# Attention and a mixture of experts in one kernel: order of the attention and item work fixed by the program, weight buffers with fixed uses

## The chip, the core and the metric

One Trainium2 chip, one core. The metric is the device time of one execution in microseconds (us). Engines: PE (TensorE, matrix products), DVE (VectorE), ACT (ScalarE), POOL (GpSimd, which issues the indirect transfers), SP (SyncE, which issues the other transfers). PEld stands for PE's weight loads.

## What is computed

```python
def _attn_ref(q, k, v, tau):            # B, N, C = 4, 3648, 256
    qn = q / (np.linalg.norm(q, axis=1, keepdims=True) + 1e-06)
    kn = k / (np.linalg.norm(k, axis=1, keepdims=True) + 1e-06)
    s = kn.transpose(0, 2, 1) @ qn / tau
    s = s - s.max(-1, keepdims=True)
    a = np.exp(s)
    a /= a.sum(-1, keepdims=True) + 1e-09
    return (v @ a).astype(np.float32)
...
g_idx = np.argmax(x @ w_group, axis=1)  # x: 14592 x 256; 4 groups of 4 experts
...
h = np.maximum(xg[mask_e] @ w1[g, e], 0.0)      # 256 -> 1024
ye = h @ w2[g, e]                               # 1024 -> 256
out[tok_idx] = combined[:, None] * ye
```

Attention is over channels: the score matrix of a batch is 256 x 256, summed over 3648 rows. Each row of its output is a token; the token goes to the best expert of its best group, weighted by both softmax values. Everything is float32.

## The kernel before, in words

**Attention.** A batch is 28 tiles of 128 rows and a remainder of 64; four tiles make a unit, so a batch has 8 units (`GPB`), the last with the remainder alone, and the kernel 32. For a unit of scores, `s_load` brings q and k, `s_split` splits one of the four tiles (`SPLIT`) into a rounded part and its rest and squares all of them on ACT (`sq`), `s_mm` multiplies into `sacc` (L207), and `s_add` adds the squares on DVE (`sqa`). The split tile takes three products of rounded values (`qkhi`, `qklo`) where the other tiles take one full-precision product. For a unit of output, `x_load` brings v, `x_tr` transposes it on PE (`vtr`, L284), ACT rounds it to `vth`, DVE forms the rest `vtl`; `x_mm` makes six products a tile (`xmm`, L303) with the softmax matrix (`ahi`, `alo`), and ACT copies them to `xs`, a ring of ten buffers. The softmax matrix is widened by 20 columns, so that the same products give the routing logits `L`.

**Softmax and routing** are chains of small instructions that go from engine to engine, written as generators. `softmax(b)`: DVE sums the squares (`ssq`), PE sums over partitions (`nps`), ACT takes the root, DVE scales the scores, ACT the exponential, PE transposes (`atp`) and multiplies with the routing weights (`awp`), ACT and DVE make `ahi` and `alo`. `routing(b, j0, j1)` takes a range of tiles (`RANGES`): DVE finds group and expert, counts by a scan (`inc`, `rs`), PE sums the counts over partitions (`pp`, L359), DVE forms slot numbers `si`; `scatter` then lets POOL write each tile's 128 tokens to their slots in `x_sorted` (L405), 116 in all, with a `pause` (L139) behind each.

**Order.** The loop over `t` issues unit t of the scores and unit t - 10 of the output (`XOFF`); from t = 32 on only output is left. A step of a generator is issued at four places a loop (`sstep`) or by `advance`. Up to t = 31 only POOL takes the program's order; the other engines' order is made by a list scheduler, which places instructions by priority. From t = 32 to step 2 of the items all engines take the program's order, and behind that SP and POOL alone.

**Items.** An item is one expert with 512 tokens; there are 28 (`NBIG`), and the 24 from item 4 on (`host`) also carry a quarter of a group of smaller token blocks (`qmm`, `qacc`). The first `KPRE` = 4 items come from an early table (`tables_pre`), made once the first two batches and the range before `PRE` are counted; the others from `tables_rest`, when every token is counted. SP fetches an early item's rows with a plain transfer, POOL those of the others with a gather (`gather`, L478), for which all scatters and the clearing of the empty slots (L557) must be done. Weights of 1 MB (w1, w2) and of 512 KB (for the small blocks) go through a ring of three raw buffers (`raw_tile`); ACT and DVE split them into `wh` and `wl` (`split_w`). An item has eight steps f: `ffn1` makes six products into `hmm` (L793), ACT and DVE make `hh` and `hl`, and `ffn2` multiplies those of two steps ago (`lag`) into `yacc` (L809). POOL sends the results out (L819). Rows of early items are transposed on PE (`split_x`), those of the others on DVE (`turn_x`), both during the item before.

## Time and profile before

| | us |
|---|---|
| median of 3 runs | 962.31 (960.9 to 963.89) |
| the profiled execution | 958.63 |
| its span, first to last instruction | 956.9 |
| PE busy | 924.3 |
| DVE busy | 750.0 |
| ACT busy | 477.3 |
| POOL busy | 332.2 |

The span has four stages by time: scores alone to about 57 us, scores and output side by side to about 200, output alone to about 252, items to 945. Busy time of an engine is the time in which it executes an instruction; an engine with idle time before an instruction waited for another engine or for a transfer, and the views name which.

### The profile page before, as it was taken

Reading aid. Unit: us, or ns where it says so; the run is one execution under the profiler, and the core shown is the slowest. Engines: PE = TensorE matmul, PEld = TensorE weight load, DVE = VectorE, ACT = ScalarE, POOL = GpSimd, SP = SyncE. Lnnn points to the kernel's source line nnn. Section 1 sums busy time; section 2 is a strip of 40 time slices with the busy share of each in tenths; the row PEclk is TensorE's granted clock in tenths of the full one; section 3 lists DMA queues with packets and bytes.
Section 4 is the critical chain, followed back from the end, with each engine's and each line's share of the span. In section 5 each row is a group of like instructions: output and inputs, shape, how many; then the busy total and the mean of one; then the engine's idle time right before and its main releaser. Section 6 shows DMA issues by size and latency. Waiting matters only on the chain.

```text
span 956.9 us, 17625 instructions
## 1 busy us (share of the span) xinstructions
PE 924.3 (97%) x6238; PEld 809.5 (85%) x6238; DVE 750.0 (78%) x1511; ACT 477.3 (50%) x748; POOL 332.2 (35%) x425
## 2 busy tenths in 40 slices
PE   7999999988899999999999999999999999999995
PEld 6889899878799988888888888888888888888884
DVE  6989978798899977777877777778777877887731
ACT  6777768447554444444444444444443444444421
POOL 0003878878787322222111311232223222322121
PEclk9999999999999999999999999999999999999998
DMA  8866778448684545555566555666666666556500
GB/s 314 313 243 224 238 269 295 144 147 287 202 296 153 176 159 210 208 210 211 213 219 212 202 213 204 222 229 221 222 223 230 222 222 220 197 212 211 200 25 26
DMA packets 105585, 201.90 MB, mean 211 GB/s; under 512 B 10035, under 2 KB 64059, under 8 KB 105488
## 3 DMA queue, kind: packets, MB, share of 16 engines
q1 hardware_dynamic: 89056, 156.12, 47.6%
q0 software_dynamic: 14944, 44.54, 12.1%
q8 instruction: 51, 0.84, 0.3%
q14 instruction: 46, 0.38, 0.1%
q10 hardware_dynamic: 1488, 0.02, 0.1%
HBM read 170.33 MB, written 31.39 MB: 211 GB/s over the span
## 4 chain that ended last, share of the span: by engine, by line
PE 80%; DVE 6%; POOL 4%; issue 4%; DMA 2%; ACT 2%; POOLq 0%; SPq 0%; DVEq 0%; ACTq 0%
PE yacc L809 32%; PE hmm L793 32%; PE sacc L207 7%; POOL x_sorted L405 3%; PE qacc L913 2%; PE qmm L896 2%; PE xmm L303 2%; DMA qkraw<-in_k 2%; DVE sqa L191 1%; POOL pad L139 1%; PE vtr L284 1%; DMA x_sorted<-xs,si 1%; DVE vtl L286 1%; ACT sq L183 1%; PE qtr L903 1%
## 5 line engine op out<-in xcount | busy, mean ns | idle before, releaser
L797 ACT ACTIVATE hh<-hmm 128x512 fp32r<-128x512 f32 x224 | 133.4, 596 | 298.0 <-PE hmm L793 284.5
L819 POOL DMA_INDIRECT out<-ys,ids x112 | 111.1, 992 | 479.1 <-ACT ys L816 449.1
L809 PE MATMUL yacc<-wh,hh 128*128 128x256 f32 x896 | 256.2, 286 | 0.1
L809 PE MATMUL yacc<-wh,hl 128*128 128x256 f32 x896 | 252.5, 282 | 0.0
L809 PE MATMUL yacc<-wl,hh 128*128 128x256 f32 x896 | 252.0, 281 | 0.0
L798 DVE SCALAR_TENSOR_TENSOR hl<-hmm,hh 128x512 fp32r<-128x512 f32 x224 | 153.4, 687 | 85.9 <-ACT hh L797 84.3
L809 PEld LDWEIGHTS yacc<-wh,hh 128*128 128x128 f32 x896 | 168.7, 188 | 24.4 <-issue 15.0
L793 PE MATMUL hmm<-xth,wh 128*128 128x512 f32 x448 | 177.3, 396 | 0.0
L793 PE MATMUL hmm<-xth,wl 128*128 128x512 f32 x448 | 177.0, 395 | 0.0
L793 PE MATMUL hmm<-xtl,wh 128*128 128x512 f32 x448 | 176.8, 395 | 0.0
L809 PEld LDWEIGHTS yacc<-wl,hh 128*128 128x128 f32 x896 | 169.0, 189 | 8.2
L687 DVE STREAM_TRANSPOSE xt<-xg 32x256 f32<-32x256 f32 x384 | 167.2, 435 | 6.5 <-DMA xg<-x_sorted,ix_big 0.2
L640 DVE TENSOR_TENSOR wl<-wraw,wh 128x1024 fp32r<-128x1024 f32 x112 | 134.9, 1223 | 46.9 <-ACT wh L639 45.6
L809 PEld LDWEIGHTS yacc<-wh,hl 128*128 128x128 f32 x896 | 168.5, 188 | 0.0
L405 POOL DMA_INDIRECT x_sorted<-xs,si x116 | 135.6, 1169 | 56.3 <-issue 29.3
L639 ACT ACTIVATE wh<-wraw 128x1024 fp32r<-128x1024 f32 x112 | 116.2, 1055 | 74.1 <-DMA wraw<-in_moe_w 50.5
L793 PEld LDWEIGHTS hmm<-xth,wl 128*128 128x128 f32 x448 | 84.1, 188 | 19.9
L793 PEld LDWEIGHTS hmm<-xtl,wh 128*128 128x128 f32 x448 | 84.2, 188 | 11.0 <-DVE xtl L668 0.3
L793 PEld LDWEIGHTS hmm<-xth,wh 128*128 128x128 f32 x448 | 84.2, 188 | 9.7
L207 PE MATMUL sacc<-qkraw 128*128 128x256 f32 (+1 forms) x352 | 85.2, 388 | 6.0 <-DMA qkraw<-in_k 6.0
L207 PEld LDWEIGHTS sacc<-qkraw 128*128 128x128 f32 (+1 forms) x352 | 65.0, 193 | 14.6 <-DMA qkraw<-in_q 5.9
L303 PE MATMUL xmm<-ahi,vth 128*128 128x276 f32 (+1 forms) x232 | 69.7, 302 | 3.2 <-ACT ahi L263 1.8
(233 smaller groups left out, 1212.3 us busy)
## 6 DMA issues: line engine op xcount, KB each, us to landing
wraw<-in_moe_w SPq DMA_DIRECT2D x56, 1024.0 KB, 7.2
wraw<-in_moe_w SPq DMA_DIRECT2D x96, 512.0 KB, 5.4
vr<-in_v SPq DMA_DIRECT2D x28, 512.0 KB, 4.2
qkraw<-in_q SPq DMA_DIRECT2D x27, 512.0 KB, 4.8
qkraw<-in_k SPq DMA_DIRECT2D x27, 512.0 KB, 5.7
xg<-x_sorted SPq DMA_DIRECT2D x4, 544.0 KB, 4.0
x_sorted<-xs,si POOLq DMA_INDIRECT x116, 4.0
out<-ys,ids POOLq DMA_INDIRECT x112, 3.6
```

The costliest lines, as they stand in the source:

```text
L207: PE.matmul(d["acc"][:, c, :], kt[:rows, 1, cs], qt[:rows, 0, :], start=d.pop("first", True) and c == 0, stop=(g == NG), skip_group_check= ...
L303: PE.matmul(mm[:rows, :NE], vt[:, c, j * P:j * P + rows], at[:, c, :], start=(n == 0), stop=(n == 5))
L405: ins = POOL.indirect_dma_start(out=xs_d, out_offset=bass.IndirectOffsetOnAxis(ap=si[:rows, j:j + 1], axis=0), in_=xs[:rows, t, 0:RW].bitc ...
L639: ACT.activation(whs[n][:, s], raw[:, s], AF.Copy)
L640: DVE.tensor_tensor(wls[n][:, s], raw[:, s], whs[n][:, s], ALU.subtract)
L687: ins = DVE.transpose(xt[qs_, :, :, rs], xg[:, :, :, qs_])
L793: PE.matmul(mm, wt[:, c, fs], xt[:, c, :], start=(n == 0), stop=(n == 5))
L797: d["hh"] = ACT.activation(hh, mm, AF.Relu)
L798: d["hl"] = DVE.scalar_tensor_tensor(hl, mm, 0.0, hh, ALU.max, ALU.subtract)
L809: PE.matmul(a, ht[:, tsl], wt[:, f, :], start=(f == 0 and t % 2 == 0 and n == 0), stop=(f == 7 and n == 2), skip_group_check=True)
L819: ins = POOL.indirect_dma_start(out=out, out_offset=bass.IndirectOffsetOnAxis(ap=d["ids"][:, t:t + 1], axis=0), in_=ys[:, t, :], in_offset ...
L896: PE.matmul(mm[r, :], qs["xT"][q % 2][:, c, r], qs["w", p][:, c * 512:(c + 1) * 512], start=(c == 0), stop=(c == 1), tile_position=(0, p * ...
```

## The change

All five engines take the program's order from the start to the end of the items. The loop over attention is a list of steps (t, x): output starts at t = 13 (`FIRST`), two steps with output alone stand after t = 13 and t = 15 (`ALONE`), and unit 31 of the output, the short one, goes before unit 30. Within a step, tiles of scores and output alternate, and behind each a `hook` counts; a generator's `yield n` waits for n hooks. Softmax goes into one line of generators (`small`), routing and tables into another (`rgens`); `take` and `give` hand the one small PSUM buffer around. Squares and their additions are halved and placed between tiles. Units 9 to 12 don't split a tile. Softmax adds its squares instead of reducing, makes the column norms as four single columns and spreads one of them by a product with a diagonal matrix (`dq`), and scales scores on ACT. Logits are copied by ACT.

The items keep their products. `KPRE` is 3, `PRE` (2, 16), batch 2 is routed in three ranges, item 3 is fetched by a gather and still transposed on PE, and outputs are held (`outs`) until the first gathers are issued. Raw buffers have fixed uses: from item 4 on, both weights of an item go through buffer 0 and the small blocks' through 1 and 2. `PLAN` says what DVE and ACT do for the next item behind `ffn1` (0) and `ffn2` (1) of each step.

```diff
-KPRE = 4
+KPRE = 3
+FLIP = 4
...
-RANGES = [[(0, 16), (16, NJ)], [(0, 16), (16, NJ)], [(0, 16), (16, 20), (20, NJ)], [(0, 16), (16, NJ)]]
+RANGES = [[(0, 16), (16, NJ)], [(0, 16), (16, NJ)], [(0, 8), (8, 16), (16, NJ)], [(0, 16), (16, NJ)]]
...
-PRE = (2, 20)
+PRE = (2, 16)
...
+VLOADS = 3
+UNSPLIT = (9, 10, 11, 12)
...
-XOFF = GPB + 2
-TM = US
-TURNS = (0, 1, 2, 3)
+FIRST = GPB + 5
+ALONE = (13, 15)
+HOP = 4
+MANUAL = 24
...
+    hooks, held = [0], [False, 0]
+
+    def take():
+
+        if held[0] or hooks[0] < held[1]:
+            return False
+        held[0] = True
+        return True
+
+    def give(n):
+        held[:] = [False, hooks[0] + n]
...
     def softmax(b):
...
+        hop = HOP if b in (0, B - 1) else HOP + 2
+        sqa = d["sqa"]
         ssq = ap_.tile([P, 2, C], F32, name="ssq", bufs=1)
-        DVE.tensor_reduce(ssq, d["sqa"].rearrange("p t j c -> p t c j"), AX.X, ALU.add)
-        yield
+        DVE.tensor_tensor(sqa[:, :, 0:2, :], sqa[:, :, 0:2, :], sqa[:, :, 2:4, :], ALU.add)
+        DVE.tensor_tensor(ssq, sqa[:, :, 0, :], sqa[:, :, 1, :], ALU.add)
+        yield hop
+        ACT.activation(tmp1, onesf[:, 0:1], AF.Sqrt)
+        while not take():
+            yield 1
...
+        for i in range(4):
+            PE.matmul(nps[:, C + i:C + i + 1], ssq[:, i // 2, (i % 2) * P:(i % 2 + 1) * P], onesf[:, 0:1],
+                      start=(i == 0), stop=True, skip_group_check=True)
+        rn = ap_.tile([P, 4], F32, name="rn4", bufs=1)
+        ACT.activation(rn, nps[:, C:C + 4], AF.Sqrt)
+        ACT.activation(tmp1, zero[:, 0:1], AF.Exp)
+        give(2)
+        yield 1
...
+        dq = ap_.tile([P, 2, P], F32, tag="rn", name="dq", bufs=1)
+        DVE.tensor_tensor(dq, ident.unsqueeze(1).broadcast_to([P, 2, P]),
+                          rn[:, 0:2].unsqueeze(2).broadcast_to([P, 2, P]), ALU.mult)
+        yield hop
+        while not (d.get("scored") and take()):
+            yield 1
+        nps = ps.tile([P, 512], F32, tag="misc", name="nps", bufs=1)
+        PE.matmul(nps[:, 0:C], onesf, dq.rearrange("p c n -> p (c n)"), start=True, stop=True, skip_group_check=True)
         sm = ap_.tile([P, 2, C], F32, name="sm", bufs=1)
         for c in range(2):
-            DVE.scalar_tensor_tensor(sm[:, c, :], d["acc"][:, c, :], rn[:, C + c:C + c + 1], rn[:, 0:C],
-                                     ALU.mult, ALU.mult)
+            ACT.activation(sm[:, c, :], d["acc"][:, c, :], AF.Copy, scale=rn[:, 2 + c:3 + c])
+        yield 1
+        DVE.tensor_tensor(sm, sm, nps[:, 0:C].unsqueeze(1).broadcast_to([P, 2, C]), ALU.mult)
+        give(hop)
...
             DVE.tensor_scalar(ax[:, c, 0:C], sm[:, c, :], se[:, c:c + 1], None, ALU.mult)
-        yield
-        yield
+        yield hop
+        while not take():
+            yield 1
...
         DVE.tensor_copy(ax[:, :, C:NE], awp[:, 0:2 * NL].rearrange("p (c n) -> p c n", c=2))
+        give(hop)
+        yield 2
         ahi = ap_.tile([P, 2, NE], F32R, name="ahi")
         alo = ap_.tile([P, 2, NE], F32R, name="alo")
         ACT.activation(ahi, ax, AF.Copy)
+        yield 1
         DVE.tensor_tensor(alo, ax, ahi, ALU.subtract)
+        yield 2 if b < B - 1 else 1
         d["ahi"], d["alo"] = ahi, alo
```

The line of routing, the raw buffers, the hooks and the loop over attention:

```diff
+        yield 2
+        ez = wide("ez", NL)
+        ACT.activation(ez, z, AF.Exp)
+        yield HOP if (b, j0) < (2, 16) else HOP + 3
+        while not take():
+            yield 1
...
+    turn = [0]
+
+    def raw_tile(n=None):
+
+        n = turn[0] % 3 if n is None else n
+        turn[0] += 1
+        return wp.tile([P, 2048], F32, tag=f"wraw{n}", name="wraw", bufs=1)
...
-        d[which + "r"] = t = raw_tile().rearrange("p (c f) -> p c f", c=n)
+        d[which + "r"] = t = raw_tile(0 if turn[0] > 9 else None).rearrange("p (c f) -> p c f", c=n)
...
-    ms.enter_context(tc.manual_schedule(engines={ET.Pool}))
-
-    rgens = []
+    ms.enter_context(tc.manual_schedule(engines={ET.Pool, ET.SP, ET.Activation, ET.PE, ET.DVE}))
...
+    class Line:
...
+                if r is not None:
+                    self.wait = r
+                    return
+                self.gens.pop(0)
+
+        def hook(self):
+            self.wait -= 1
+            if self.wait <= 0:
+                self.step()
+
+    small, rgens = Line(), Line()
+    wp = tb_pre = tb_big = tb_pc = tb_sub = nsub = None
...
+    def hook():
+        hooks[0] += 1
+        small.hook()
+        rgens.hook()
...
+    steps, x = [], 0
+    for t in range(US):
+        steps.append((t, x if t >= FIRST else None))
+        x += t >= FIRST
+        if t in ALONE:
+            steps.append((None, x))
+            x += 1
+    steps += [(None, u) for u in (*range(x, UX - 2), UX - 1, UX - 2)]
...
+    for n, (t, x) in enumerate(steps):
+        nx = steps[n + 1][1] if n + 1 < len(steps) else None
+        if t is not None and t + LOADS < US:
...
+        if x is not None and x % GPB == 0:
+            while "alo" not in st[x // GPB]:
+                small.hook()
+        if x == UX - 4:
+            while wp is None:
+                hook()
+            fetch_x(items[0], tb_pre, 0)
+        while x is not None and pend_of(x - RING + (x >= UX - 4)):
+            hook()
+            scatter(2)
         if nx is not None:
-            with ahead(t >= US):
-                x_tr(nx)
...
+            x_tr(nx, 0)
+        done = len([a for a in steps[:n + 1] if a[0] is not None])
+        upto = min(US - 1, done + (n >= FIRST))
+        for j in range(GJ):
+            if t is not None and j < rows_of(t % GPB)[1]:
+                s_tile(t, j)
+                if t % GPB == NG:
+                    st[t // GPB]["scored"] = True
+                hook()
+            if j == 0 and nx is not None:
+                x_tr(nx, 1)
+                hook()
+            if x is not None and j < rows_of(x % GPB)[1]:
+                x_tile(x, j)
+                hook()
+            if j == (2 if x is not None else 0) and t is not None and t + 1 < US:
+                s_split(t + 1)
+            if j == 1 and x == UX - 2:
                 split_x(items[0])
...
+            if j % 2 == 0 and squares and squares[0][0] <= upto:
+                s_square(*squares.pop(0))
+            if j % 2 == 1 and adds and adds[0][0] <= upto:
+                u, h = adds.pop(0)
+                s_add(u, h)
+                if h and u % GPB == NG:
+                    small.gens.append(softmax(u // GPB))
+                    small.step()
+            if fetched is None and wp is not None:
+                fetched = n
+            if fetched is not None and n >= fetched + 2 and x != UX - 1 and j % 2 and quarters:
+                split_w(0, *quarters.pop(0), of=4)
```

The items:

```diff
+        outs.append((d, t))
+        if fetched is None:
+            send()
...
-        if i < KPRE:
-            fetch_x(d, tb, k)
         if weights:
             fetch_big(i, "w1")
             fetch_big(i, "w2")
-        if i >= KPRE:
+        if i != KPRE + 1:
             fetch_x(d, tb, k)
...
+    rgens.gens += [routing(B - 1, *RANGES[B - 1][-1]), tables_rest()]
...
-        t = raw_tile()
+        t = raw_tile(1 + half)
...
+    PLAN = {(0, 0): range(0, 2), (0, 1): range(2, 4), (1, 0): ("w1", 0), (2, 0): ("w1", 1), (2, 1): range(4, 7),
+            (3, 0): range(7, 9), (3, 1): range(9, 12), (4, 0): range(12, 14), (4, 1): range(14, 16),
+            (5, 0): ("w2", 0), (5, 1): ("w2", 1), (6, 0): "x", (6, 1): "ids"}
+
+    def ready(i, f, half):
+
+        what = PLAN.get((f, half))
+        if what == "x":
+            split_turned(items[i])
+        elif what == "ids":
+            ids_of(items[i])
+        elif isinstance(what, tuple):
+            split_w(i, what[0], (what[1],))
+        elif what:
+            turn_x(items[i], what)
+
...
-                if i + 2 == KPRE:
-                    advance(1000)
-                    scatter(NJ)
-                    tb_big, tb_pc, tb_sub, nsub = tables_rest()
-                get(i + 2, weights=jn is None)
+                if i + 2 != KPRE:
+                    get(i + 2, weights=jn is None)
...
             ffn1(items[i], f)
+            if quarters:
+                split_w(0, *quarters.pop(0), of=4)
+            if FLIP <= i + 1 < NBIG:
+                ready(i + 1, f, 0)
...
+        if n == 8 * KPRE - 2:
+            split_x(items[KPRE])
+        if n < len(seq) and FLIP <= seq[n][0] + 1 < NBIG:
+            ready(seq[n][0] + 1, seq[n][1], 1)
...
+        hook()
+        if n == 15:
+            while tb_big is None:
+                advance(1)
+        if tb_big is not None and fetched is not None:
+            get(KPRE)
+            fetch_x(*where(KPRE + 1))
+            fetched = None
+            send()
+        scatter(8)
```

**First place of the order: PE, the routing product `pp` and the transposes `atp` of batch 3's softmax, shortly after the last unit of scores.** `vtr` are transposes of v, `xmm` output products, `tri` and `onesb` the constant operands of `pp`. Before:

```order
L303 MATMUL xmm<-ahi,vtl 128x276
L284 MATMUL vtr<-ident,vr 128x64 x2
L359 LDWEIGHTS tri
L359 MATMUL pp<-rs,tri 128x16
L360 LDWEIGHTS onesb
L360 MATMUL pp<-rs,onesb 128x16
L248 MATMUL atp<-ident,ax 128x128 x4
L303 MATMUL xmm<-ahi,vth 128x276
```

After:

```order
L351 MATMUL xmm<-alo,vth 128x276
L409 LDWEIGHTS tri
L409 MATMUL pp<-rs,tri 128x16
L410 LDWEIGHTS onesb
L410 MATMUL pp<-rs,onesb 128x16
L351 MATMUL xmm<-ahi,vth 128x276
...
L333 MATMUL vtr<-ident,vr 128x64 x2
...
L351 MATMUL xmm<-ahi,vtl 128x276
L351 MATMUL xmm<-alo,vth 128x276
L296 MATMUL atp<-ident,ax 128x128 x4
L351 MATMUL xmm<-ahi,vth 128x276
```

`pp` and `atp` stood one behind the other, right behind two transposes; now 12 output products, two transposes and 12 more products stand between them, and the left-out rows are those products.

**Second place: POOL, from the last scatters to the first gathers (`xg`) of items that come from the late table.** `zero` clears the empty slots, `out` is the output, `qxg` the small blocks. Before:

```order
L404 IOTA xs 128x1
L405 DMA x_sorted<-xs,si 238080x272
L139 MEMSET pad 128x256
L819 DMA out<-ys,ids 14592x256 x8
L557 DMA x_sorted<-zero,endi 238080x272
L478 DMA xg<-x_sorted,ix_big 128x1088
L819 DMA out<-ys,ids 14592x256 x4
L478 DMA xg<-x_sorted,ix_big 128x1088
L478 DMA qxg_4538<-x_sorted,ix_pc 128x272
```

After:

```order
L458 IOTA xsr 128x1
L459 DMA x_sorted<-xsr,si 238080x272
L145 MEMSET pad 128x256
L617 DMA x_sorted<-zero,endi 238080x272
L535 DMA xg<-x_sorted,ix_big 128x1088 x2
L933 DMA out<-ys,ids 14592x256 x12
L535 DMA xg<-x_sorted,ix_big 128x1088
L535 DMA qxg_4578<-x_sorted,ix_pc 128x272
```

Eight outputs stood between the last scatter and the clearing; now the clearing and two gathers follow the last scatter, and twelve outputs come behind them.

## Rows read from the trace of the kernel before

**Rows 1.** The page: the span, and busy time of PE (us, share, instructions).
```profile
span 956.9 us, 17625 instructions
...
PE 924.3 (97%) x6238; PEld 809.5 (85%) x6238; DVE 750.0 (78%) x1511; ACT 477.3 (50%) x748; POOL 332.2 (35%) x425
```

**Rows 2.** Stages: length, busy PE, PEld, DVE, ACT, POOL (instructions), clock, DMA share, GB/s.
```profile
57.00:200.00 143.00, 136.95 (x951) 128.07 (x950) 121.28 (x246) 99.05 (x177) 94.46 (x135) 1.00 0.66 223
200.00:252.00 52.00, 43.74 (x319) 40.43 (x317) 44.37 (x148) 31.01 (x72) 41.40 (x69) 0.97 0.64 213
280.00:945.00 665.00, 664.91 (x4526) 571.23 (x4524) 512.22 (x972) 289.85 (x434) 167.54 (x172) 1.00 0.57 200
```

**Rows 3.** Waits of PE: waiting line, awaited line, us in all, times, longest.
```profile
PE pp L359 <- DVE rs L357: 4.8, 6, 1.6
PE vtr L284 <- DVE vtl L286: 2.4, 3, 1.3
PE xmm L303 <- ACT ahi L263: 1.8, 1, 1.8
PE xmm L303 <- ACT xs L306: 1.4, 2, 0.9
```

**Rows 4.** The chain that ended last, attention: start us, us, what.
```profile
5.97 29.36 PE sacc L207 x145
...
120.85 3.08 PE xmm L303 x24
...
124.81 3.30 PE sacc L207 x18
```

**Rows 5.** Timeline of PE, 45 to 47 us: start us, us, instruction.
```profile
45.60 1.04 PE L284 MATMUL vtr<-ident,vr 128*128 128x128 f32 x8
46.40 0.36 PE L207 MATMUL sacc<-qkhi 128*128 128x256 f32 x1
```

**Rows 6.** Groups by line, 0 to 252 us: small products, busy us and mean ns.
```profile
L257 PE MATMUL awp<-wcat,aT 128*128 128x20 f32 x32 | 4.1, 262 | 0.1
...
L248 PE MATMUL atp<-ident,ax 128*128 128x128 f32 x16 | 3.3, 310 | 1.8 <-DVE ax L242 1.1 <-DVE carry L364 0.6
```

**Rows 7.** The same chain, the first item.
```profile
251.97 3.06 PE hmm L793 x12
...
263.78 1.44 PE yacc L809 x12
...
269.44 1.44 PE yacc L809 x12
```

**Rows 8.** Timeline of PE, 208 to 211 us.
```profile
208.25 0.43 PE L303 MATMUL xmm<-alo,vth 128*128 128x276 f32 x1
...
210.78 0.36 PE L303 MATMUL xmm<-ahi,vth 128*128 128x276 f32 x1
```

**Rows 9.** Timeline of POOL: scatters, the clearing of empty slots, the first gather.
```profile
85.95 2.26 POOL L405 DMA_INDIRECT x_sorted<-xs,si  x1 [19.48 <-DVE si L372]
...
189.40 1.00 POOL L405 DMA_INDIRECT x_sorted<-xs,si  x1 [0.28 <-POOL xs L402]
...
190.89 0.98 POOL L405 DMA_INDIRECT x_sorted<-xs,si  x1 [0.16 <-issue]
...
297.98 0.94 POOL L405 DMA_INDIRECT x_sorted<-xs,si  x1 [1.77 <-issue]
...
310.59 0.90 POOL L557 DMA_INDIRECT x_sorted<-zero,endi  x1 [0.30 <-DVE ids L491]
315.84 1.06 POOL L478 DMA_INDIRECT xg<-x_sorted,ix_big  x1 [4.34 <-DVE tst L458]
```

**Rows 10.** DMA issues: KB each, median us from issue to landing.
```profile
wraw<-in_moe_w SPq DMA_DIRECT2D x56, 1024.0 KB, 7.2
...
xg<-x_sorted,ix_big POOLq DMA_INDIRECT x24, 7.9
```

**Rows 11.** Timeline of PE, the last product.
```profile
944.98 0.28 PE L809 MATMUL yacc<-wh,hl 128*128 128x256 f32 x1
```

More of the change, by code (lines that the diff above doesn't have):

```diff
@@ L307, in x_mm @@
[L307 to L312 removed]
+        if j == 0:
+            rows_at[b, g] = ring(GJ, NE, name="xs") if g < NG else rp.tile([P, 1, NE], F32, name="xsr", bufs=2)
+        xs = rows_at[b, g]
+        mm = ps.tile([P, 512], F32, tag="mm", name="xmm", bufs=3)
+        n = 0
+        for c in range(2):
+            for vt, at in ((x["th"], d["ahi"]), (x["tl"], d["ahi"]), (x["th"], d["alo"])):
+                PE.matmul(mm[:rows, :NE], vt[:, c, j * P:j * P + rows], at[:, c, :],
+                          start=(n == 0), stop=(n == 5))
+                n += 1
@@ L314, in bc @@
+        ACT.activation(xs[:rows, j, :], mm[:rows, :NE], AF.Copy)
+        if j == nj - 1:
+            ACT.activation(d["L"][:rows, g * GJ:g * GJ + nj, :], xs[:rows, :nj, C:NE], AF.Copy)
+    scatters, pend, now, rows_at, early, gone = [], [], [0], {}, [], set()
     def bc(x, n):
@@ L539, in tables_rest @@
         DVE.tensor_tensor(small, small, r, ALU.mult)
+        yield 1
         nb = r16("nb")
```

450 lines of the change are left out of this document (207 added, 243 removed).

## The prediction

> **What bounds the kernel now.** I read four views: the page's shares, the stages, the waits of PE, and the chain with the timeline for the pace of single products.
>
> The page shows PE busy for 924.3 us of a span of 956.9 [rows 1]. That average covers stages with different limits. From 280 to 945 us, the items, PE is busy 664.91 of 665 us: nothing that moves a wait can gain there. From 57 to 200 us, attention with scores and output side by side, it is busy 136.95 of 143, so 6.05 us are idle; from 200 to 252 us, where only the output half of attention is left, 43.74 of 52, so 8.26 us are idle [rows 2]. These 14.3 us are what a better order can win back for certain. DVE is the next engine, with 121.28 busy of 143.
>
> The waits say who causes them [rows 3]: the small product `pp` of the routing stands behind DVE's `rs` for 4.8 us in six places, the transposes of v behind DVE's `vtl` for 2.4, the first `xmm` of a batch behind ACT's `ahi` for 1.8, `xmm` behind ACT's evacuation `xs` for 1.4. So PE waits mostly where a link of a chain of small instructions stands directly behind the link that feeds it.
>
> A second estimate comes from the pace of the products. A full unit of scores takes 3.30 us, its 24 output products 3.08 [rows 4], its eight transposes 46.40 - 45.60 = 0.80 [rows 5]. 28 full units make 28 x 7.18 = 201.0; the four remainders are one tile instead of four, a quarter of 7.18 each, 7.2 together. The six groups of small products (softmax and routing) are led by 4.1 and 3.3 us of busy time [rows 6]; the others are smaller, so together at most 4.1 + 5 x 3.3 = 20.6, and since their records overlap perhaps half. With item 0's eight transposes (0.8) PE has 219 to 230 us of work between its first product at 5.97 and the first product of item 0 at 251.97 [rows 4, 7]. That stretch is 246.0 us, so 16 to 27 us of it are not work; I take the middle, 21.
>
> One piece of it has no wait: from 208.25 to 210.78 [rows 8] eleven intervals of `xmm` take 2.53 us, 0.23 each, against 3.08 / 24 = 0.128 elsewhere. [...]
>
> **The change, part by part.**
>
> *Order of attention.* All five engines now follow the program. Output of batch b starts later against its scores (13 units behind, then 11 after two output-only steps, instead of 10), and the links of softmax and routing are released one by one between products ("hooks"). The first order excerpt shows it: `pp` and `atp` stood in a row, now 12 output products, two transposes and 12 more stand between. 12 products of 0.128 are 1.5 us, about the longest single wait on `rs` (1.6) [rows 3]. I therefore take the waits on `rs`, `ahi` and the like as gone, half of the 2.4 on `vtl` as staying, because the transposes still follow each other through two PSUM buffers, and all of the 1.4 on `xs`: 14.3 - 1.2 - 1.4 = 11.7 us gained. Bounds: 0 and 14.3.
> [...]
> *The rest of the 21*: 21 - 14.3 - 1.3 = 5.4 us of slower pace without a named wait. I take half, 2.7; bounds 0 and 11 (27 minus the same).
> *Moved work.* Squares and their additions are cut in half and given places; copying the logits goes from DVE to ACT; the reduction of four square sums becomes two additions. DVE loses work and ACT gains some; neither is PE's, and ACT is busy 99.05 of 143 [rows 2], so I cost this at nothing. If that cover is gone, it shows as PE waiting for ACT's `xs`.
> *Added products.* Four units no longer split their last tile (two full-precision products for six rounded ones), the norms take five products for three, and batch 2 is routed in three ranges instead of two. Nearest rows: 4.1 us for 32 records of `awp` [rows 6], 0.13 each; some 20 more records are 2 to 3 us if nothing is saved, 0 if the dropped ones weigh as much. I take 1.0.
> *The strict order itself.* DVE is busy 85% of 57 to 200 us [rows 2] and would be nearer 90% in a shorter stage, so a link can come later than its place. PE waited 1.6 us at worst for `rs` [rows 3] with ready products behind it; links that stand 1.5 us or more apart leave little of that, so I cost the fixed places themselves at nothing, and the other outcome is a rival below. [...]
>
> *Item 3's rows.* Three instead of four items come from the early table, so item 3 now waits for every scatter. The second excerpt shows POOL: the late rows of an item are now fetched before any output is sent, where eight outputs stood ahead. PE needs item 3's rows at the second-last step of item 2, 22 steps of 2.83 us after the first `hmm` ((269.44 - 263.78) / 2) [rows 7], so 62 us later: 251.97 - 15.7 + 62 = 298. When do they come? Scatters follow each other every 190.89 - 189.40 = 1.49 us at best; 116 of them from 85.95 end at 259 plus some 5 for their 28 iotas; before they ended at 298.9 because POOL also waited for routing [rows 9]. From the clearing of the empty slots at 310.59 to the gather at 315.84 are 5.3 us, and a gather lands 7.9 us after its issue [rows 9, 10]. Arrival: 264 + 13 = 277 at best, 299 + 13 = 312 with POOL's old timetable. The wait is 0 to 14 us; with routing earlier by the gain above, POOL's timetable lies near the middle (295), so I take 1.5.
>
> *Items.* From item 0 on PE gets the same products in the same sequence; 2.83 us a step stays [rows 7], and DVE and ACT have room beside it (512.22 and 289.85 of 665 [rows 2]). *End:* the last product at 944.98 [rows 11] and the 12 us to the end of the span are untouched.
>
> Sum: -11.7 - 1.3 - 2.7 + 1.0 + 1.5 = -13.2 us. The profiled execution took 958.63 us (span 956.9); the median shown is 962.31, 3.7 higher. I apply the difference to the median: 962.3 - 13.2 = 949.1 us (against the profiled execution 945.4).
>
> **The rivals.**
>
> *The scatters set the pace.* POOL keeps most of its old timetable, item 3's rows come at about 306, and PE waits 8 us instead of 1.5: 949 + 7 = 956 us. For it: POOL is busy 94.46 of 143 and 41.40 of 52 [rows 2], the most loaded it ever is. Against: it also waited for routing, which comes earlier.
>
> *Nothing gained: one late operand holds the queue.* [...] The waits vanish at `pp` and come back at `xs` and `vtl`: the 13 us are given back, 962 us, give or take 4. For it: DVE's 85%. [...] Against: the waits of DVE and ACT on each other are not in PE's list now.
>
> *Slower: one raw buffer for both weights of an item.* Now w1 and w2 of the items beside small tokens go through the same raw buffer. w2's load can start only when w1's second half has been split at step 2, and is needed at step 5: three steps, 8.5 us [rows 7], against 7.2 us from issue to landing [rows 10]. PE itself is two steps ahead of its need, 5.7 us more. It decides from a landing of 14 us on, twice the median, which would take two loads queueing behind each other. A wait of 1 us in each of 24 items makes +24: 949 + 24 = 973 us. Against it: loads of 7.2 us.
>
> **How the numbers follow.** Forecast 949.1: chance 0.68. Scatters 956: 0.16. Nothing gained 962: 0.09. Slower 973: 0.07. About 0.3% (2.9 us, so 959.4 and 965.2) is what a measurement of this kernel can tell from no change. The forecast is faster (0.68); of the scatters' case 0.13 is faster, 0.03 lies within; of the third 0.02 is faster, 0.05 within, 0.02 slower; the fourth is slower. Sum: faster 0.83, same 0.08, slower 0.09. Range: all waits gone and all slower pace recovered is 14.3 + 1.3 + 11 = 26.6 less 1 = 25.6, so 937 at the low end; the high end takes in the scatters' case and its bound, 960.
>
> **What would show it.** Right: first `hmm` near 236; 57 to 252 us with PE idle under 4 us until then; no wait on `rs` or `ahi` in PE's list; granted clock 1.00 throughout; item steps still 2.83; 28 items in the same 693 us. Wrong: a wait at item 3's transposes or first products (scatters), long waits on `xs` or `vtl` (queue), ACT's `wh` waiting for `wraw` with `hmm` standing behind (buffer).

## The result, and the profile after

The changed kernel takes 949.17 us (median of 4 runs, 948.94 to 950.34); before, with one run more, 962.07 (960.9 to 963.89). The ratio is 0.9867, 95% interval 0.9849 to 0.9884. Forecast were 949.1 us, and 937 to 960.

The two profiled executions are nearer to each other: 949.24 against 958.63, 9.4 us, where the medians differ by 12.9. The profiled execution of before is none of the four whose times are listed, and it is quicker than all of them. The other 3.5 us are the subject of the first experiment.

The page of the changed kernel, span and busy time [rows 1]:

```profile
span 947.5 us, 17624 instructions
...
PE 924.7 (98%) x6246; PEld 809.5 (85%) x6246; DVE 749.5 (79%) x1502; ACT 484.1 (51%) x822; POOL 336.1 (35%) x426
```

Its stages, columns as in [rows 2], the later cuts moved to where these stages now end:

```profile
57.00:200.00 143.00, 140.72 (x980) 131.15 (x979) 115.62 (x254) 108.87 (x229) 84.07 (x128) 1.00 0.66 231
200.00:236.00 36.00, 33.76 (x264) 31.93 (x263) 29.89 (x97) 25.54 (x68) 30.62 (x53) 1.00 0.63 209
236.00:280.00 44.00, 43.30 (x284) 38.92 (x284) 41.78 (x110) 25.36 (x47) 38.60 (x62) 1.00 0.67 229
280.00:930.00 650.00, 650.00 (x4422) 557.26 (x4421) 518.43 (x970) 282.08 (x424) 177.37 (x169) 1.00 0.60 205
```

PE is idle for 2.28 us from 57 to 200 (6.05 before) and for 2.24 us from 200 to 236, and the granted clock is 1.00 in all four stages; 0.97 is gone. The items are as full as they were. The waits of PE that are left [rows 3]:

```profile
PE vtr L333 <- DVE vtl L335: 2.7, 4, 1.6
PE pp L409 <- DVE rs L401: 1.3, 3, 0.5
PE atp L296 <- DVE carry L414: 0.8, 1, 0.8
...
PE xmm L351 <- ACT xs L354: 0.2, 1, 0.2
```

`rs` fell from 4.8 to 1.3, `xs` from 1.4 to 0.2, `ahi` is gone; `vtl` stays, 2.7 for 2.4. The chain of waits of this execution reaches back only to 922 us, so PE's timeline has to give the stages' ends [rows 7, 11]: the first product of item 0, then the last product.

```profile
243.41 0.40 PE L897 MATMUL hmm<-xth,wh 128*128 128x512 f32 x1
```
```profile
936.31 0.28 PE L913 MATMUL yacc<-wh,hl 128*128 128x256 f32 x1
```

First `hmm` in the timeline is at 243.41 (before 251.81; the chain's entry at 251.97 begins 0.16 later), the last product at 936.31 instead of 944.98: 8.4 of the 9.4 us came from before the first item, 0.3 from the items, and 0.7 from behind the last product (11.2 us to the end of the span for 11.9). POOL, from the last scatter to the first gather [rows 9], and item 3's transposes on PE:

```profile
296.13 0.94 POOL L459 DMA_INDIRECT x_sorted<-xsr,si  x1 [1.98 <-issue]
...
297.56 0.93 POOL L617 DMA_INDIRECT x_sorted<-zero,endi  x1 [0.16 <-DVE tp L490]
301.39 1.05 POOL L535 DMA_INDIRECT xg<-x_sorted,ix_big  x1 [2.90 <-issue]
```
```profile
307.51 1.04 PE L764 MATMUL xtr<-ident,xg 128*128 128x128 f32 x8
```

Item 3's rows are transposed right when PE gets there. The first four items take 90.59 us (before 91.27), the other 24, up to the start of the last product, 602.31 (601.90).

### The profile page after: what moved, and what is told of

Its sections match the earlier page's. It is cut to its first block, busy times and chain, and to the rows that moved or that the text cites. A ratio compares the mean times of both kernels' runs of the same rounds, so it can differ in the third digit from the quotient of the medians.

```text
span 947.5 us, 17624 instructions
## 1 busy us (share of the span) xinstructions
PE 924.7 (98%) x6246; PEld 809.5 (85%) x6246; DVE 749.5 (79%) x1502; ACT 484.1 (51%) x822; POOL 336.1 (35%) x426
## 5 line engine op out<-in xcount | busy, mean ns | idle before, releaser
L933 POOL DMA_INDIRECT out<-ys,ids x112 | 128.0, 1143 | 453.8 <-ACT ys L920 422.8
L736 DVE TENSOR_TENSOR wl<-wraw,wh 128x1024 fp32r<-128x1024 f32 (+1 forms) x116 | 134.8, 1186 | 15.5 <-ACT wh L735 15.5
L459 POOL DMA_INDIRECT x_sorted<-xs,si x112 | 122.3, 1092 | 64.9 <-DVE qklo L182 38.1
L735 ACT ACTIVATE wh<-wraw 128x1024 fp32r<-128x1024 f32 (+1 forms) x116 | 115.5, 1023 | 0.5 <-DMA wraw<-in_moe_w 0.5
L224 PE MATMUL sacc<-qkraw 128*128 128x256 f32 (+1 forms) x368 | 93.1, 389 | 6.4 <-DMA qkraw<-in_k 6.4
L224 PEld LDWEIGHTS sacc<-qkraw 128*128 128x128 f32 (+1 forms) x368 | 66.9, 194 | 14.6 <-DMA qkraw<-in_q 6.0
L351 PE MATMUL xmm<-ahi,vth 128*128 128x276 f32 (+1 forms) x232 | 75.7, 326 | 0.2 <-ACT xs L354 0.2
```

Source lines behind the costliest of these rows:

```text
L224: PE.matmul(d["acc"][:, c, :], kt[:rows, 1, cs], qt[:rows, 0, :], start=d.pop("first", True) and c == 0, stop=(g == NG), skip_group_check= ...
L351: PE.matmul(mm[:rows, :NE], vt[:, c, j * P:j * P + rows], at[:, c, :], start=(n == 0), stop=(n == 5))
L459: ins = POOL.indirect_dma_start(out=xs_d, out_offset=bass.IndirectOffsetOnAxis(ap=si[:rows, j:j + 1], axis=0), in_=xs[:rows, t, 0:RW].bitc ...
L735: ACT.activation(whs[n][:, s], raw[:, s], AF.Copy)
L736: DVE.tensor_tensor(wls[n][:, s], raw[:, s], whs[n][:, s], ALU.subtract)
L933: ins = POOL.indirect_dma_start(out=out, out_offset=bass.IndirectOffsetOnAxis(ap=d["ids"][:, t:t + 1], axis=0), in_=d["ys"][:, t, :], in_o ...
```

## The experiments

Kernels of one group ran on the same chip. Times are medians in us, ratios are to the kernel before on that chip; the last three columns are from the profile: the start of the first `hmm`, then the length of items 0 to 3 and of items 4 to 27, up to the start of the last product.

| kernel | us | ratio (95%) | hmm | 0-3 | 4-27 |
|---|---|---|---|---|---|
| before, shown | 962.07 | | 251.81 | 91.27 | 601.90 |
| changed, shown | 949.17 | 0.9867 (0.9849 to 0.9884) | 243.41 | 90.59 | 602.31 |
| *group 1* b_again | 964.51 | 0.9998 (0.9970 to 1.0026) | 255.47 | 92.48 | 606.29 |
| a_again | 953.73 | 0.9883 (0.9856 to 0.9909) | 244.40 | 92.86 | 602.67 |
| a_nohop | 1018.86 | 1.0563 (1.0534 to 1.0592) | 301.56 | 99.44 | 603.42 |
| b_order | 1036.9 | 1.0735 (1.0705 to 1.0765) | 327.74 | 92.74 | 605.04 |
| *group 2* a_sched | 963.54 | 0.9946 (0.9912 to 0.9981) | 246.58 | 97.90 | 603.25 |
| a_lag | 983.67 | 1.0156 (1.0084 to 1.0227) | 268.81 | 94.29 | 603.22 |
| a_ring | 965.1 | 0.9938 (0.9898 to 0.9978) | 254.40 | 94.58 | 606.44 |
| a_spread | 961.8 | 0.9915 (0.9890 to 0.9939) | 248.00 | 97.68 | 603.38 |
| *group 3* a_ctl | 948.74 | 0.9866 (0.9836 to 0.9896) | 242.71 | 90.45 | 602.31 |
| a_nopause | 947.69 | 0.9855 (0.9825 to 0.9884) | 241.70 | 90.44 | 602.35 |
| a_r1 | 948.45 | 0.9860 (0.9831 to 0.9890) | 244.02 | 90.44 | 602.35 |
| *group 4* a_kpre4 | 956.47 | 0.9898 (0.9868 to 0.9927) | 247.53 | 91.61 | 604.15 |

The kernel before took 965.7, 970.0, 961.79 and 967.06 us on the four chips. In groups 2 and 4 the changed kernel itself wasn't run; there kernels of the group are compared, or a trace is read by itself, and a difference to the changed kernel on another chip is only a hint.

### Both kernels once more: b_again, a_again

No edit.

> The kernel before once more, unchanged, for a second profile of it. Theory A (the profiled execution of before was a quick one of an unsteady kernel): the runs lie at 960 to 964 again, and this profile shows first hmm 1 to 4 us later than 251.97, with the extra time as waits of PE in attention, the items again in 693 us. Theory B (the 3.5 us between that profile and its median lie elsewhere, in the items or outside the span): first hmm within 0.5 us of 251.97, and the items or the time around the span longer.

> The changed kernel once more, unchanged. Theory A (fixed places make the time steady): first hmm within 0.5 us of 243.41, all runs within 1.5 us of 949.2. Theory B (its runs only happened to agree): first hmm moves by 1 us or more, runs spread over 3 us or more as those of before do.

Before: its runs lie at 960.4 to 971.93, not within A's 960 to 964, and this execution loses 3.7 us in attention (first `hmm` 255.47) and 4.4 us in items 4 to 27. Of the 3.7 us, 1.8 are idle time of PE and 2.0 a longer busy time, with a granted clock of 0.94 from 200 us to first `hmm` (0.97 in the execution shown before). Theory A holds for attention in size, B for the items, which A had taken as fixed. So the kernel before does vary on one chip, by 11.5 us; whether the profiled execution shown before was quick by that or by its chip is open, as its chip is not on record. Three waits tell where the items lose. First ACT's in the execution shown before, then ACT's in this one (both from 330 to 930 us), then PE's in this one from 300 on:

```profile
ACT wh L639 <- DMA wraw<-in_moe_w: 49.4, 32, 3.3
```
```profile
ACT wh L639 <- DMA wraw<-in_moe_w: 85.9, 35, 5.1
```
```profile
PE yacc L809 <- DVE ys L818: 2.4, 4, 1.3
```

ACT's rounding of weights waits for their load, for 49.4 us in the quick execution and for 85.9 in this one. DVE's `wl` waits with ACT, 43.8 and 57.5 us (from 330 to 940 us); with a longest wait of 3.3 us none of that reaches PE, whose list from 300 us on is empty there; with 5.1 it does, and PE waits 2.4 us for `ys`. The longest of these four waits of PE, followed back in b_again on ACT, DVE and PE:

```profile
650.21 1.06 ACT L639 ACTIVATE wh<-wraw 128x1024 fp32r<-128x1024 f32 x1 [4.46 <-DMA wraw<-in_moe_w]
```
```profile
651.30 1.23 DVE L640 TENSOR_TENSOR wl<-wraw,wh 128x1024 fp32r<-128x1024 f32 x1 [4.83 <-ACT wh L639]
...
659.94 0.88 DVE L818 TENSOR_SCALAR ys<-yacc,xg 128x256 f32<-128x256 f32 x2
```
```profile
660.87 0.39 PE L809 MATMUL yacc<-wh,hh 128*128 128x256 f32 x1 [1.27 <-DVE ys L818]
```

Between the two rows of DVE it works without a wait, so the late load reaches PE by way of `wh`, `wl` and `ys`. In the three profiles of the changed kernel no such wait of ACT stands in the list. Between the profiles of b_again and a_again, on one chip, 11.1 us lie before first `hmm`, 3.6 in items 4 to 27, and items 0 to 3 are 0.4 us longer in the changed kernel.

Changed: neither theory as stated. The runs stay within 2.2 us of each other, but at another level (952.8 to 954.99); first `hmm` comes 1.0 us later, items 0 to 3 take 2.3 us longer. The place is item 3, whose first products on PE stand behind ACT's rounding of its transposed rows. The timelines of PE, then of ACT, in a_again:

```profile
314.27 0.49 PE L897 MATMUL hmm<-xth,wh 128*128 128x512 f32 x1 [1.20 <-issue]
315.00 0.50 PE L897 MATMUL hmm<-xtl,wh 128*128 128x512 f32 x1 [0.23 <-issue]
```
```profile
310.79 0.60 ACT L765 ACTIVATE xth<-xtr 128x512 fp32r<-128x512 f32 x1 [2.91 <-PE xtr L764]
313.62 0.60 ACT L765 ACTIVATE xth<-xtr 128x512 fp32r<-128x512 f32 x1 [2.24 <-remote]
```

The transposes stand at 308.51 in the records, with no wait for `xg` ahead of them, yet ACT begins only at 310.79 and 313.62. The second half of `xth` is done at 314.22, and the product that reads it starts at 314.27: that PE waits for ACT here is shown, why ACT was late is not. The trace names no releaser that explains it.

### Distance and order: a_nohop, b_order, a_sched

a_nohop (the loop that waits for a batch's matrix now runs both lines):

```diff
-                    self.wait = r
+                    self.wait = 1
...
-        held[:] = [False, hooks[0] + n]
+        held[:] = [False, 0]
...
-                small.hook()
+                hook()
```

> The changed kernel with every link of softmax, routing and tables released at the next hook instead of some hooks later: program order, lag and products stay, the distance between links goes. Theory A (the gain is distance between links): PE's waits on rs, ax, alo and the like come back, 5 to 8 us more of PE idle between 57 us and first hmm, which moves from 243.4 to 248 to 251; 954 to 957 us. Rival (program order and the larger lag do it, the distance is worth nothing): first hmm within 1.5 us of 243.4, 948 to 951 us.

b_order, an edit of the kernel before:

```diff
-        if t == TM:
+        if t == 0:
             ms.close()
             ms.enter_context(tc.manual_schedule(engines={ET.Pool, ET.SP, ET.Activation, ET.PE, ET.DVE}))
```

> The kernel before with all five engines in program order from the first unit on, nothing else changed. Theory A (order alone is not the gain; without places between products a link stands right behind the one that feeds it and holds the queue): first hmm not before 251.97, more likely 254 to 262; 961 to 972 us. Rival (the list scheduler's order was the fault, any fixed order mends it): first hmm 243 to 247, 949 to 954 us.

Waits of PE in a_nohop, then in b_order:

```profile
PE pp L409 <- DVE rs L401: 21.9, 7, 3.6
PE atp L296 <- DVE ax L289: 12.7, 4, 4.3
...
PE nps L254 <- DVE ssq L247: 3.2, 3, 2.1
```
```profile
PE pp L359 <- DVE rs L357: 41.5, 7, 8.9
PE nps L218 <- DVE ssq L215: 12.3, 4, 3.2
```

Both theories A hold, at several times the size expected. Without distances the changed kernel loses 65 us (1018.86 against 953.73), and the order alone makes the kernel before 71 us slower. `pp` waits 3.1 us for `rs` on average in a_nohop (21.9 / 7) and 5.9 in b_order (41.5 / 7), because its operand's chain was issued just ahead: in the wait of 3.65 us that ends at 94.97 in a_nohop DVE is busy for 3.33 us, mostly with the links up to `rs`. The named waits are a part only: from 57 us to first `hmm` the granted clock is low.

This stretch of a_nohop and of b_order, columns as in [rows 2]:

```profile
57.00:301.00 244.00, 204.96 (x1310) 190.21 (x1309) 162.03 (x381) 145.06 (x314) 132.88 (x206) 0.90 0.55 188
```
```profile
57.00:327.00 270.00, 213.03 (x1339) 196.23 (x1338) 182.33 (x401) 140.48 (x256) 134.02 (x201) 0.86 0.49 169
```

0.90 and 0.86 are the clocks granted there, with PE standing still for 39 and 57 us; the changed kernel's two stages from 57 to 236 us, with 2.28 and 2.24 us of idle time, have 1.00. What lowers the clock the traces don't name. That the fixed order of these two kernels needs distance is thereby shown, at 65 and 71 us; that the changed kernel's gain over the one before is distance alone is not, as no run takes back the shorter softmax chain, the halved squares or the unsplit tiles by themselves.

a_sched gives PE, ACT, DVE and SP back to the list scheduler as long as there are units of scores:

```diff
-    ms.enter_context(tc.manual_schedule(engines={ET.Pool, ET.SP, ET.Activation, ET.PE, ET.DVE}))
+    ms.enter_context(tc.manual_schedule(engines={ET.Pool}))
...
+        if t is None and n > US:
+            if not done_:
+                ms.close()
+                ms.enter_context(tc.manual_schedule(engines={ET.Pool, ET.SP, ET.Activation, ET.PE, ET.DVE}))
+                done_.append(n)
```

> The changed kernel, but while units of scores are left (up to about 194 us) only POOL takes the program's order and the list scheduler orders the other engines again, as it did before the change; lag, softmax chain, halves, KPRE and items as changed. Theory A (fixed places in program order carry the gain in attention): waits on rs, ax and vtl return in 57 to 200 us, 3 to 7 us more of PE idle there, first hmm at 246 to 250. Rival (the larger lag, the shorter chain and the unsplit tiles carry it, whoever sets the order): first hmm within 1 us of 243.4 to 244.4.

The stage from 57 to 200 us of a_sched, columns as in [rows 2]:

```profile
57.00:200.00 143.00, 139.69 (x974) 129.78 (x973) 113.64 (x254) 106.97 (x219) 88.53 (x135) 1.00 0.66 226
```

Its longest wait of PE:

```profile
PE hmm L903 <- ACT xth L765: 5.2, 1, 5.2
```

PE is idle for 3.31 us from 57 to 200, only 1.0 more than in the changed kernel (expected 3 to 7), and first `hmm` is at 246.58, in the range of A but at its edge, and ahead of a_spread's 248.00 on the same chip. So a scheduler that places by priority does nearly as well, once the larger lag and the new chain give it the room; program order isn't worth much by itself, and without distances it costs much (65 us in a_nohop). Much of the rest of its time is item 3: PE waits 5.2 us there, for ACT's rounding again and not for `xg`. Its ten runs spread over 11.4 us (960.12 to 971.5), a_spread's ten, in program order on the same chip, over 2.8 (960.68 to 963.45); a_ring's ten, in program order with the old ring, over 11.4. So neither the order alone nor the fixed buffers alone made the time steady in these runs.

### The lag: a_lag

```diff
-FIRST = GPB + 5
-ALONE = (13, 15)
+FIRST = GPB + 2
+ALONE = ()
...
-                small.hook()
+                hook()
```

> The changed kernel with the old lag: output starts 10 units behind the scores instead of 13, without the two steps of output alone; where a batch's softmax matrix isn't there yet, its links are issued one behind the other until it is. Theory A (the spread chain needs some 26 hooks, 6 to 7 steps, so places and lag belong together): the chains of batches 1 to 3 bunch up, PE waits 3 to 6 us a batch, first hmm at 252 to 262. Rival (the lag is of no account): first hmm within 2 us of 244.

Waits of PE in a_lag, on links of the two chains:

```profile
PE atp L296 <- DVE ax L289: 7.8, 3, 4.1
PE pp L409 <- DVE ax L305: 6.4, 2, 3.2
...
PE awp L303 <- ACT aT L298: 3.1, 4, 0.9
```

The chain's own links stand bare again, 17.3 us in these three rows, and first `hmm` is at 268.81, later than A's 252 to 262. Distances need the three units of lag; neither gains by itself.

### The raw buffers: a_ring

```diff
-        d[which + "r"] = t = raw_tile(0 if turn[0] > 9 else None).rearrange("p (c f) -> p c f", c=n)
+        d[which + "r"] = t = raw_tile().rearrange("p (c f) -> p c f", c=n)
...
-        t = raw_tile(1 + half)
+        t = raw_tile()
```

> The changed kernel with the raw buffers as a ring of three again, nothing else changed. Theory A (the fixed uses take the weights' arrival out of the items): ACT's wh waits for wraw return (0 in the changed kernel, 49 and 86 us in the two profiles of before), DVE's wl behind them, and the items take 0.5 to 5 us longer than 693 to 695.5. Rival (the places in PLAN do it, the buffers don't matter): no wait of wh for wraw over 5 us in all, items the same within 0.5 us. Rival of the prediction (one buffer for both weights costs time): items shorter than 693.

Waits of ACT in a_ring from 330 to 930 us, the longest that isn't for PE:

```profile
ACT hh L901 <- remote: 38.0, 7, 5.5
```

Items 4 to 27 take 606.44 us. In the ten profiles with fixed uses they take 602.3 to 604.2, in the four with a ring 601.9, 605.0, 606.3 and 606.4. A has the size right and the place wrong: no wait at `wh` came back. Nor is the wait at `hh`, put down to "remote", a loss of 38.0 us: at the same seven places ACT waits 4.7 us in a_spread too, on the same chip with fixed uses. The first of them, in a_ring and in a_spread, then PE's wait in a_ring from 330 us on:

```profile
413.62 0.60 ACT L901 ACTIVATE hh<-hmm 128x512 fp32r<-128x512 f32 x1 [5.45 <-remote]
```
```profile
409.60 0.60 ACT L901 ACTIVATE hh<-hmm 128x512 fp32r<-128x512 f32 x1 [4.72 <-PE hmm L897]
```
```profile
PE hmm L897 <- DVE xtl L785: 1.5, 3, 0.6
```

Items 4 to 27 are 3.1 us longer than a_spread's, with the same products in the same order. Set side by side product by product, 3.0 of these arise at the second and third products of items 7, 8, 11, 15, 16, 19 and 23, which need `xtl`, the rest of the item's rows, from a DVE that is 0.7 us late with all it does since such an `hh`. What holds that `hh` up the trace does not name. So the fixed uses take away a loss that comes and goes; the rival of the prediction (one buffer for both weights costs time) is out.

The rest of a_ring's time isn't the buffers' doing. Its order is that of the changed kernel on every engine, PE's products from 15 to 131 us stand at the same times within 0.02 us as in the changed kernel's first profile, and then they slip by 6.55 us between 137 and 156, before any weight is loaded (stages of a_ring, columns as in [rows 2]):

```profile
135.00:150.00 15.00, 13.10 (x88) 11.43 (x87) 10.91 (x20) 13.47 (x30) 10.18 (x19) 1.00 0.70 251
150.00:165.00 15.00, 13.64 (x70) 11.86 (x69) 11.52 (x32) 8.46 (x20) 6.51 (x10) 0.77 0.47 167
```

ACT fell behind step by step, 0.8 us at 113 and 3.45 with its `xs` at 130; a few waits of PE of 1.1 and 1.4 us followed, then a stretch at a granted clock of 0.77. What held ACT up isn't settled.

### What sets item 3's arrival: a_spread, a_nopause, a_r1, a_kpre4

a_spread, in `routing`, behind its first and second link:

```diff
-        yield 1
+        yield 2
...
-        yield 1
+        yield 3
```

> The changed kernel with the first two links of routing one and two hooks farther apart, since PE's longest wait left (1.6 to 1.8 us at 219, vtr for DVE's vtl) stands behind a row of 20 DVE instructions of routing and tables. Theory A (POOL's scatters set when item 3's rows come, so attention's next gain is given back there): the wait at 219 falls below 0.6, first hmm 1 to 2.5 us earlier, item 2 to 3 longer by as much, the time within 1 us of the changed kernel. Rival (item 3 has room): first hmm 1 to 2.5 us earlier and the time as much shorter.

POOL's timeline in a_spread, a scatter of batch 2 and the first gather:

```profile
235.21 0.98 POOL L459 DMA_INDIRECT x_sorted<-xs,si  x1 [8.83 <-issue]
...
310.89 1.06 POOL L535 DMA_INDIRECT xg<-x_sorted,ix_big  x1 [5.65 <-issue]
```

Waits of PE in a_spread, the two longest behind the start:

```profile
PE xtr L764 <- DMA xg<-x_sorted,ix_big: 4.0, 1, 4.0
PE awp L303 <- ACT vth L334: 2.4, 1, 2.4
```

The wait at 219 went and another came in its place (`awp`, 2.4 us, at 210), so no gain of first `hmm` is seen. The first gather came at 310.89, and PE waited 4.0 us for `xg` itself. That is the scatters' case of the prediction, seen bare. Chips differ (961.79 to 970.0 us for the kernel before on four), so the gather is best counted from first `hmm`: 62.9 us behind it here, 57.8 to 58.2 in the shown kernel, a_again, a_ctl, a_sched and a_ring. Of these 5 us some 2 stand at the last scatter already (54.9 us behind first `hmm`, 52.4 to 53.0 in those five), and 2.5 come between the clearing and the gather (6.6 us for 3.8 to 4.2), for which the trace names no releaser. POOL's wait of 8.8 us at 235 isn't all the edit's: the step from one scatter to the next is 10.5 us there, and in a_ring and a_sched, on the same chip with the old distances, steps of 8.5 and 8.8 us stand at 230 and 223.

a_nopause:

```diff
     def pause():
-        POOL.memset(pad, 0.0)
+        return
```

> The changed kernel without the memset of 0.33 us behind each of POOL's 116 scatters. Theory A (POOL's row of scatters decides when item 3's rows come, and in slower executions when ACT gets a buffer for xs): pitch of scatters 1.49 to about 1.1, last scatter at 265 to 285 instead of 296 to 297, first gather as much earlier; items 0 to 3 in 90.6 us without a wait at item 3's transposes; the control's excess over 90.6 us in these items is the gain, 0 to 6 us. Rival (the transfers set the pace, or scatters without a pause crowd out the loads of q, k and v): last scatter not before 292, or more waits on xs or qkraw in attention, no gain or a loss.

a_r1:

```diff
-RANGES = [[(0, 16), (16, NJ)], [(0, 16), (16, NJ)], [(0, 8), (8, 16), (16, NJ)], [(0, 16), (16, NJ)]]
+RANGES = [[(0, 16), (16, NJ)], [(0, 8), (8, 16), (16, NJ)], [(0, 8), (8, 16), (16, NJ)], [(0, 16), (16, NJ)]]
```

> The changed kernel with batch 1 routed in three ranges (8, 8 and 13 tiles) instead of two, since POOL stands still for 4.8 us at 149 until the first 16 tiles of batch 1 have slots. Theory A (POOL's pace and its waits for routing decide item 3's rows): that gap goes, last scatter 3 to 6 us earlier than the control's, item 3's wait shorter by up to as much; one routing chain more costs DVE about 4 us, of which PE sees 0 to 1. Rival (the DVE time of one more chain delays what PE waits for, or a later routing gap takes up the gain): last scatter within 1.5 us of the control's, no gain or up to 2 us of loss.

> The changed kernel once more, as the control on the chip of the next two. Theory: first hmm within 2.5 us of 243.4 to 244.4, items 4 to 27 in 602 to 603.5 us, as in every kernel with fixed raw buffers so far; the first four items 90.6 to 97 us, whatever item 3's rows cost on this chip; faster than the kernel before by 1.0 to 1.5%.

The control holds what was expected: first `hmm` at 242.71, items 4 to 27 in 602.31 us, the first four in 90.45, the ratio 0.9866. POOL's timeline in a_nopause: two scatters in a row, the last one, the gather.

```profile
188.57 0.97 POOL L459 DMA_INDIRECT x_sorted<-xs,si  x1 [0.30 <-issue]
189.85 0.99 POOL L459 DMA_INDIRECT x_sorted<-xs,si  x1 [0.31 <-issue]
...
287.08 0.93 POOL L459 DMA_INDIRECT x_sorted<-xsr,si  x1 [1.77 <-issue]
...
295.93 1.05 POOL L535 DMA_INDIRECT xg<-x_sorted,ix_big  x1 [6.71 <-issue]
```

The pitch falls from 1.49 to 1.28 us (expected 1.1), the last scatter comes at 287.1 instead of the control's 295.2 (expected 265 to 285), the gather only 4.8 us earlier (295.93 against 300.74). On this chip item 3 had no wait to lose (90.45 us in the control), and A's gain there was none, as it should be. What it did gain, 1.0 us, lies in attention: PE's wait for `vtl` 2.1 instead of 2.7, for `rs` 0.9 instead of 1.3. Its four runs (947.66 to 947.9) all lie below the control's (948.58 to 949.16): faster than both kernels, by 0.1% of the changed one. Whether it also saves item 3's wait where there is one wasn't tried.

In a_r1 the gap at 149 went, a step of 4.6 us from one scatter to the next came at 223 instead (2.6 in the control there), and the last scatter stands at 294.4, 0.8 before the control's, and the time is the control's (948.45 for 948.74 us): the rival. What POOL gains at one gap it gives back at the next wait for routing.

a_kpre4:

```diff
-KPRE = 3
+KPRE = 4
...
-RANGES = [[(0, 16), (16, NJ)], [(0, 16), (16, NJ)], [(0, 8), (8, 16), (16, NJ)], [(0, 16), (16, NJ)]]
+RANGES = [[(0, 16), (16, NJ)], [(0, 16), (16, NJ)], [(0, 8), (8, 20), (20, NJ)], [(0, 16), (16, NJ)]]
...
-PRE = (2, 16)
+PRE = (2, 20)
```

> The changed kernel with the early table as before the change: four early items, the table made once batch 2 is counted up to tile 20 instead of 16 (ranges of batch 2: 8, 12 and 9 tiles); item 3's rows come by SP's plain transfer. Theory A (the change trades item 3's early rows for an earlier table, and the trade is even on a quick chip): items 0 to 3 in 90.4 us with no wait at item 3's transposes; the table, and with it item 0's weights, one unit (4 to 7 us) later, which shows as PE waiting for wh or xg before the first products of item 0, first hmm 1 to 6 us later; 0 to 5 us slower than the changed kernel where that has no wait at item 3, even or faster where it has. Rival (the table has that much room): first hmm within 1 us of 242.7 to 244.4, time the same or less by item 3's wait.

The table comes only 1.1 us later than in the kernel as shown (`tb_pre` at 223.51 against 222.43), yet first `hmm` is at 247.53. What the list shows as late are DVE's and ACT's operands.

Waits of PE in a_kpre4:

```profile
PE vtr L333 <- DVE vtl L335: 3.9, 2, 2.4
...
PE xmm L351 <- ACT xs L354: 1.0, 2, 0.8
```

`vtl` 3.9 us instead of 2.7, a granted clock of 0.97 from 200 to 252, and item 0's first rounded weights at 235.37 instead of 231.77. A's sign and size (1 to 6 us) hold, as far as another chip can tell, its reason only in part: no wait of PE for `wh` or `xg` stands in the list. Item 3 has no wait, as A had it, but items 4 to 27 take 604.15 us, which isn't explained. Its ratio, 0.9898, lies above the changed kernel's three (0.9866 to 0.9883), within the intervals' reach.

## Why the prediction was right, and where it wasn't

**The whole.** The time is as forecast, by the difference to the median of before, but in part by luck. By the profiled execution, against which the sum was made, the step "Sum: -13.2 us" is too large: 9.4, with first `hmm` at 243.41 and not "near 236", PE idle for 5.2 us until then, not "under 4", and 1.3 us of waits on `rs` left. Of the prediction's signs the granted clock and the 693 us of the items came true. The 3.5 us that bring the median to its place lie where the sum has nothing: the kernel before varies more (11.5 us over b_again's ten runs, 2.2 over a_again's four), and its profiled execution stood outside its timed runs. How the 3.5 us divide between attention, the items and the chip is not shown.

**Order of attention** (11.7 of 14.3): PE's idle time from 57 us to first `hmm` fell from 14.3 to 5.2 (186.4 us, 181.17 busy), so 9.1. The step that waits on `rs` and `ahi` "are gone" was right for `ahi` and for three quarters of `rs`; half of `vtl` was taken as gone, and none of it is: rows of routing and tables now stand at fixed places ahead of it on DVE, and the longest of these waits went when a_spread moved them apart. `xs`, taken as staying, went.

**Lower clock and slower pace, less the added products** (1.3 + 2.7 - 1.0 = 3.0): from first product to first `hmm`, before and after, columns as in [rows 2]:

```profile
5.97:251.81 245.84, 231.53 (x1545) 213.90 (x1545) 209.13 (x444) 171.55 (x290) 135.68 (x203) 0.99 0.70 244
```
```profile
6.05:243.41 237.36, 231.79 (x1553) 213.86 (x1553) 193.34 (x426) 180.33 (x362) 121.18 (x190) 1.00 0.70 246
```

This stretch became 8.5 us shorter, and PE's busy time in it 0.3 longer, so these three together are -0.3, not 3.0. The 0.97 went as said (1.00 in all four stages after); "the rest of the 21" was mis-sized. No run shows the 1.3 us of the sum: in the trace of before, the eleven intervals from 208.25 to 210.78 us, at a granted clock of 0.50, took 1.1 us more than at the pace elsewhere. Of 245.84 us before, 14.3 were idle and 1.1 went there, 15.4 in all, just under the lower bound of "16 to 27": the estimate of 219 to 230 us of work was right at its upper end alone, and the middle, 21, gave the sum a reserve that busy time doesn't show. The added products were counted wrongly too: batch 2 was routed in three ranges before as well, and the trace has 8 records more (1553 for 1545), not some 20.

**Item 3's rows** (1.5, bounds 0 to 14): item 3 takes 0.2 us more in the shown execution (22.79 for 22.59), without a wait of PE. The gather came at 301.39 and landed 4.2 us later, at 305.6 where the sum had 295; but PE got there at 307.51, not at 298, since first `hmm` was later too. So the rows were there 2 us ahead of PE because both times moved by some 10 us, which is luck and no merit of the 1.5. The trace has PE waiting for `xg` where the gather came at 310.89, 4.0 us in a_spread. The 2.3 us of a_again and the 5.2 of a_sched stand behind ACT's rounding and are not shown to be the rows'.

**Items** (nothing): nearly right for the shown pair, where only `pp`'s wait in item 0 went (20.78 us for 21.73), wrong for the other profiles with a ring: items 4 to 27 take 3.1 us longer in a_ring than in a_spread and 3.6 longer in b_again than in a_again. The prediction had the fixed buffers only as a rival on the slower side.

**The rivals.** "Nothing gained: one late operand holds the queue" did not happen here; PE held by late operands is what a_nohop and b_order show, with 21.9 and 41.5 us of waits on `rs` before `pp`, in kernels 65 and 71 us slower. The prediction let the row of distances ("links that stand 1.5 us or more apart leave little of that") decide against it, and that was the right reason. "The scatters set the pace" was seen in a_spread alone, whose edit made the scatters later. "One raw buffer" fell: no wait on it, landing of the 1 MB loads 6.0 us in the median (7.2 before [rows 10]), as the transfers of the changed kernel show:

```profile
wraw<-in_moe_w SPq DMA_DIRECT2D x56, 1024.0 KB, 6.0
```

## What to carry to other kernels

In these runs a fixed order helped only with distance (65 us lost without it in a_nohop, 71 in b_order): between a link of a small chain and the link it feeds, place as much other work on the waiting engine as the chain takes, and give the lag between producer and consumer stages room for all these distances (first `hmm` at 268.81 in a_lag, without that room). Before a sum is made against one profiled execution, ask whether it is typical: a time that lies outside its own kernel's runs says that something varies, and a change can win by taking that away. Where a queue of many small transfers runs through several stages, look for all that waits at its end; here the same row of POOL set an item's arrival (PE waited 4.0 us for `xg` in a_spread) and cost attention 1.0 us (a_nopause).

## What had not been expected of the hardware

PE's products in two executions of one instruction order, the shown one and a_ring's, agreed within 0.02 us for 116 us, while ACT fell 3.45 us behind, and then parted by 6.55 us (from 137 to 156); in a_ring's 15 us from 150 on the granted clock was 0.77, for 1.00 in the shown one. And a memset of 0.33 us on POOL behind each scatter, which PE never waits for, cost 1.0 us of PE's time in attention.
